# Hash-masked attention and a gated feed-forward layer on one core: bits by DVE, a third of a norm on ACT, casts and turns moved

## The chip, the cores and the metric

The kernel runs on one core of a Trainium2 chip. The metric is the time of one execution on the device, in microseconds (us), median of several runs. Five engines work side by side, each in the order of its own queue: PE (matrix products; its weight loads are PEld in the profile), DVE and POOL (element work), ACT (functions and scaled copies), and SP, which only issues transfers here. An engine waits only for the data and the buffers that its next instruction needs; what stands behind that instruction in its queue waits with it.

## The reference

Attention over 4 batches of 8 heads, 768 positions and 64 dimensions. Each position of q and k gets 6 bits, the signs of its products with a 64x6 matrix; a query sees only the keys with the same 6 bits.

```python
q_bits = (np.einsum('bhsd,dk->bhsk', q, proj) > 0)
k_bits = (np.einsum('bhsd,dk->bhsk', k, proj) > 0)
mask = q_bucket[:, :, :, None] == k_bucket[:, :, None, :]
scores = np.where(mask, scale * np.matmul(q, k.transpose(0, 1, 3, 2)), -1e9)
attn = softmax(scores)                       # with 1e-9 in the denominator
x = np.matmul(attn, v)                       # heads side by side: 3072 x 512
xn = x / np.sqrt(np.mean(x * x, -1) + 1e-6) * rms_g
g, val = xn @ w_gate, xn @ w_val             # 512 x 1536 each
out = (g * sigmoid(g) * val) @ w_out         # 1536 x 512
```

## The kernel before

The 4 batches are cut into 8 units u of 384 queries (u = 2b and 2b + 1), with 8 heads h each. A head's work is three *steps*: in step t PE computes the scores of two key blocks of the next step (`scores`, s_ps, L321), ACT takes exp of those of this step (`probs`, psb, L333), and then whatever the plan holds for the step is issued, in the order in which it was entered. There are 192 such steps. The order of heads starts with heads 0 and 1 of units 0 and 1, then heads 2 to 7 of unit 0, then of unit 1, then unit by unit; so unit 0's last head is done in step 32, and batch 1's first heads begin at step 48. The plan is a table written by hand (`at(w, s, f, ...)`: window w of 24 steps, step s), and the feed-forward products of a unit are spread by weights over the steps of the next one (`spread`).

The bits enter the scores as 6 further rows of the operands in `QK`: rows 64 to 69, of a size such that an unlike bit pushes the score down and exp makes it nothing. They come in four steps. `turn_pe` transposes a head's q or k on PE (t_ps, L148) and DVE copies it (kT, qT, L150); `cast_part` casts it into QK (L164, on POOL, or on DVE for one half of q). `hash_direct` multiplies by the 64x6 matrix for a pair of heads (d_ps, L222); `sign` takes the signs on DVE (bits, L211), once for each half of the columns. Then `send` moves the bits to the rows of QK by DMA from SP's queue (L261), two transfers a head, or `move` does it on DVE (L252), two copies a head. The bits lie in two buffers in turn, so the signs of one pair wait for the transfers of the pair before the last. Pairs 1 to 3 of batch 0 start at steps 2, 8 and 14 (`s0`), with the hash at s0 + 4; the pairs (b, hp) = (1, 0) and (1, 1) have a row of step numbers each. Later pairs are loaded as blocks of 32 columns, turned on DVE (`turn_dve`, L174 and L181), cast on POOL (`cast_pool`, L194) and hashed by `hash_one` (L202); `spots` holds their steps: load, k's turns, q's turns, hash. A helper puts off POOL's casts and v's that would come due in steps 2 to 6 of a window:

```python
def behind_norm(t):
    return t - t % NS + 7 if 2 <= t % NS < 7 else t
```

v is cast to 16 bits into `vl` (`v_prep`, L290; for pairs 1 to 3 of batch 0 on DVE). Loads of q, k and v share eight buffers, taken in turn, so that a load waits for the cast or the turn that frees its buffer, and SP's later transfers wait behind it.

`av` multiplies exp's results with v (o_ps, L346; one buffer in PSUM, two heads). After an odd head `attn_out` (`o_step`) copies o_ps out on DVE (otmp, L360), takes the reciprocal (rcp, L365), and multiplies to x (L367) and squares it (sq, L372) on POOL, or on DVE for unit 0's last pair; `sumsq` (`s_step`) sums the squares (ssp, L376). At the end of a unit `norm_scale` sums over the heads (ss, L388) and raises to the power -1/2 on POOL (rstd, L392), and `norm` scales x in three thirds of 128 rows (xn, L401). `turn_x` transposes each third as a chunk on PE (x_ps, L408) and puts it out times rms_g, on DVE (xnT, L414) or as four scalings on ACT (L412). Then come the gate and value products (g_ps and v_ps, L425), tanh on ACT (t, L433), two products on DVE (a, ht, L442 and L443), and the output projection (y_ps, L454). For unit 0 this first norm stands in steps 32 and 33 and its transposes in step 37 (`TX`), with three zero matmuls (`idle`, z_ps, L515) ahead of them; later units' norms stand in step 4 of their window. t_ps, d_ps, x_ps, g_ps, v_ps, y_ps and the sums of v (m_ps, L306, put out as cvb, L309) share three PSUM buffers in turn.

Of the kernel before, what the change touches and what calls it, by code (L numbers as in the profile page):

```python
# [33 lines left out]
def kernel(  # L34
# [12 lines left out]
    nc = tc.nc  # L47
# [110 lines left out]
    def turned(b, hp, which):  # L158
        return (qT if which == "q" else kT)[b, hp].rearrange("p (h c) -> p h c", h=2)
# [48 lines left out]
    def signs(dst, ps):  # L208

        upper = ps.bitcast(U16).rearrange("p (c two) -> p c two", two=2)[:, :, 1]  # L210
        nc.vector.tensor_scalar(  # L211
            out=dst.bitcast(U16), in0=upper, scalar1=SIGN, scalar2=BIT,
            op0=ALU.bitwise_and, op1=ALU.bitwise_or,
        )

    def hash_pairs(srcs):


        pss = [bank("d_ps", [128, HALF]) for _ in range(2)]
        for t, src in enumerate(srcs):  # L220
            for e in range(2):
                nc.tensor.matmul(  # L222
                    pss[e][32 * t : 32 * t + 32, :],
                    pj[64 * e : 64 * e + 64, 6 * e : 6 * e + 32],
                    src[64 * e : 64 * e + 64],
                    start=True, stop=True, tile_position=(64 * e, 32 * t),
                )
        return pss

    def hash_direct(b, hp, heads):  # L230

        where = [(which, hh) for hh in heads for which in "kq"]
        pss = hash_pairs([turned(b, hp, which)[:, hh, :] for which, hh in where])
        bt = spool.tile([128, S], FP16, name="bits")

        def sign(e):
            signs(bt[:, e * HALF : (e + 1) * HALF], pss[e])

        def direct(which, e):
            t = where.index((which, heads[0]))
            o = (0 if which == "q" else S) + e * HALF
            signs(
                QK[b, 2 * hp + heads[0], "h"][D:KROWS, o : o + HALF],
                pss[e][32 * t : 32 * t + 6],
            )

        def move(hh):
            for which in "kq":  # L250
                t, o = where.index((which, hh)), 0 if which == "q" else S
                nc.vector.tensor_copy(  # L252
                    QK[b, 2 * hp + hh, "h"][D:KROWS, o : o + S], bt[32 * t : 32 * t + 6, :]
                )

        def send(only=heads):
            for t, (which, hh) in enumerate(where):
                if hh not in only:
                    continue
                o = 0 if which == "q" else S  # L260
                nc.sync.dma_start(  # L261
                    out=QK[b, 2 * hp + hh, "h"][D:KROWS, o : o + S],
                    in_=bt[32 * t : 32 * t + 6, :],
                )

        return sign, direct, move, send
# [46 lines left out]
    x, xn, xnT = {}, {}, {}  # L313
# [69 lines left out]
    rstds = {}  # L383

    def norm_scale(u):

        ss = spool.tile([128, 3], FP32, name="ss")
        nc.vector.tensor_reduce(  # L388
            out=ss, in_=ssp[u % 2].rearrange("p h c -> p c h"), op=ALU.add, axis=AX.X
        )  # L390
        rstd = spool.tile([128, 3], FP32, name="rstd")
        nc.gpsimd.tensor_tensor(out=rstd, in0=ss, in1=mhalf, op=ALU.pow)  # L392
        rstds[u] = rstd

    def norm(u):
        if u not in rstds:
            norm_scale(u)
        rstd = rstds.pop(u)
        xn[u] = npool.tile([128, 3, DMODEL], FP16, name="xn")
        for c in range(3):  # L400
            nc.vector.tensor_scalar_mul(xn[u][:, c, :], x[u][:, c, :], rstd[:, c : c + 1])  # L401

    def turn_x(u, c, act=False):
        if c == 0:
# [128 lines left out]
    def at(w, s, f, *a):  # L533
        plan[NS * w + s].append(lambda: f(*a))
# [7 lines left out]
    _, direct, _, _ = hash_direct(0, 0, (0,))  # L542
# [7 lines left out]
    _, direct1, _, _ = hash_direct(0, 0, (1,))  # L550
# [5 lines left out]
        direct("q", 1)  # L556
        direct1("q", 1)

    pair_signs, moves, sends = {}, {}, {}

    def hash_only(b, hp):
        pair_signs[b, hp], _, moves[b, hp], sends[b, hp] = hash_direct(b, hp, (0, 1))

    def hash_signs(b, hp):
        for e in range(2):
            pair_signs[b, hp](e)

    def hash_pair(b, hp):
        hash_only(b, hp)
        hash_signs(b, hp)  # L570

    def send_pair(b, hp, heads=(0, 1)):
        sends[b, hp](heads)
# [7 lines left out]
    for hp, s0 in ((1, 2), (2, 8), (3, 14)):  # L581
        at(0, s0, new_pair, 0, hp)
        at(0, s0, turn_pe, 0, hp, 0, "k")
        at(0, s0 + 1, turn_pe, 0, hp, 1, "k")
        at(0, s0 + 1, cast_pool, 0, hp, "k")
        at(0, s0 + 2, turn_pe, 0, hp, 0, "q")
        at(0, s0 + 3, turn_pe, 0, hp, 1, "q")
        at(0, s0 + 3, cast_part, 0, hp, "q", 0, 0, 2, nc.vector)
        at(0, s0 + 3, cast_part, 0, hp, "q", 1)
        at(0, s0 + 4, hash_pair, 0, hp)  # L590
        if hp == 1:
            at(0, s0 + 5, send_pair, 0, hp, (1,))
            at(0, s0 + 5, move_head, 0, hp, 0)
        else:
            at(0, s0 + 5, send_pair, 0, hp)
    at(0, 1, load_natural, nc.sync, 0, 3, "k")
    at(0, 1, load_natural, nc.sync, 0, 3, "q")
    at(0, 2, load_v, nc.sync, 0, 2)
    at(0, 2, load_v, nc.sync, 0, 3)
    at(0, 8, v_prep, 0, 1, nc.vector)  # L600
    at(0, 13, v_prep, 0, 2, nc.vector)
    at(0, 19, v_prep, 0, 3, nc.vector)
    for hp, t in enumerate((4, 16, 21, 31)):
        at(0, t, v_mean, 0, hp, 2, range(6))
    for i, t in enumerate((22, 34)):
# [3 lines left out]
        at(0, 39 + 3 * i, load_w, wo, moe_w_out, 6 * i, 6)  # L609


    for hp, ts in ((0, (8, 22, 23, 24, 25, 24, 26, 26, 28, 42)), (1, (17, 27, 28, 29, 30, 29, 41, 32, 33, 43))):
        tl, ts = ts[0], ts[1:]
        for w in "kq":
            at(0, tl, load_natural, nc.sync, 1, hp, w)
        at(0, tl, load_v, nc.sync, 1, hp)
        at(0, ts[0], new_pair, 1, hp)
        for t, hh, w in zip(ts[0:4], (0, 1, 0, 1), "kkqq"):
            at(0, t, turn_pe, 1, hp, hh, w)
        at(0, ts[4], cast_pool, 1, hp, "k")  # L620
        at(0, ts[5], cast_pool, 1, hp, "q")
        if hp == 0:
            at(0, ts[6], hash_pair, 1, hp)
            at(0, ts[7], send_pair, 1, hp)
        at(0, ts[8], v_prep, 1, hp)
        at(0, ts[8], v_sum, 1, hp)

    spots = {
# [11 lines left out]
    TX = 37  # L640
# [9 lines left out]
    for n, (u, h) in enumerate(order):  # L650
        for part in range(2):
            at(0, 3 * n + 4 + part, av, u, h, part)
        if h % 2:
            if (u, h) == (0, H - 1):

                at(0, 3 * n + 5, o_step, u, h // 2, nc.vector)
                at(0, 3 * n + 5, s_step, u, h // 2)
                at(0, 3 * n + 5, norm_scale, u)
                at(0, 3 * n + 6, hash_only, 1, 1)
                at(0, 3 * n + 6, hash_signs, 1, 1)  # L660
                at(0, 3 * n + 6, norm, u)
                at(0, TX + 1, send_pair, 1, 1)
                at(0, TX - 1, idle, 2, bank)
                at(0, TX, idle, 1, bank)
                for c in range(3):
                    at(0, TX, turn_x, u, c, c == 1)
                continue
            at(0, 3 * n + 5, o_step, u, h // 2)
            at(0, 3 * n + (10 if h < 7 else 7), s_step, u, h // 2)
# [35 lines left out]
    for u in range(7):  # L705
        gates = [
            (FEED, f is gate and part == 0, [(0, f, u, ft, part)])
            for ft in range(NF) for f in (gate, value) for part in range(2)
        ]
        if u == 0:  # L710
            t0 = TX + 1
            spread(t0, 2 * NS - t0, gates)
            continue
        t0 = NS * (u + 1)
        at(0, t0 + 4, norm, u)
        pieces = []
        for i in range(9):
            c, n = divmod(i, 3)
            steps = [(0, project, u - 1, c, 4 * n, 4 * n + 4)]
            if n == 2:  # L720
                steps.append((1, store, u - 1, c))
            pieces.append((4 * PROJ, True, steps))
            if i in (6, 7):
                pieces += [
                    (TURN, False, [(0, turn_x, u, c)]) for c in ((0,), (1, 2))[i - 6]
                ]
        spread(t0, NS, pieces + gates)
# [35 lines left out]
    for c in range(2):  # L763
        project(6, c, 0, NF)
        store(6, c)
    norm(7)
    project(6, 2, 0, 4)
    for c, f0, f1 in ((0, 4, 7), (1, 7, 9), (2, 9, NF)):
# [41 lines left out]
```

## Time and profile before

| | us |
|---|---|
| median of 3 runs | 339.19 (338.9 to 339.55) |
| the profiled execution | 339.4 |
| its span, first to last instruction | 337.6 |
| PE busy in it | 329.3 (98%) |
| DVE, ACT, POOL busy | 235.8, 224.0, 149.2 |
| PE waiting for the bits' transfer, first 120 us | 1.1, once |
| PE waiting for otmp, first 120 us | 0.5, once |

The page gives each engine's busy time, the chain of work that ended last, and the costliest groups of instructions. A row of a timeline gives start, duration, engine, line, operation and tiles, and in brackets how long the engine had been idle and what ended that. Matmuls are pipelined and their ends modelled: PE may be shown busy while its next weights wait, which shows in the rows of PEld. The granted clock was 1.0 all through.

### The profile page before, as it was taken

What the parts mean: (1) busy time and instruction counts of PE and PEld (TensorE: products, weight loads), DVE (VectorE), ACT (ScalarE), POOL (GpSimd) and SP (SyncE); (2) the same over time, 40 slices, a digit from 0 to 9 for tenths busy, and PEclk for the clock granted to TensorE, in tenths of its full rate; (3) what the DMA queues carried; (4) which work ended last, traced back from release to release, by engine and by line L of the source; (5) the groups of instructions that cost most, each with busy time, mean ns of one, the idle gap of its engine ahead of it and who ended that gap; (6) DMA issues with size and microseconds to landing.
All of it is one profiled execution on the core that took longest, in us unless ns stands there. A gap on an engine that the chain in (4) does not pass through costs nothing.

```text
span 337.6 us, 7795 instructions
## 1 busy us (share of the span) xinstructions
PE 329.3 (98%) x3004; PEld 198.3 (59%) x3004; DVE 235.8 (70%) x492; ACT 224.0 (66%) x325; POOL 149.2 (44%) x201
## 2 busy tenths in 40 slices
PE   8898999999999999999999999999999999999996
PEld 4566756655566555655656556565656666664554
DVE  2898696777869558875788658884776446674870
ACT  2788886666677767777667667776667767754322
POOL 3457949427553632746373523738371121112000
PEclk9999999999999999999999999999999999999999
DMA  7944899982818527070816118000200010001002
GB/s 234 328 142 150 129 152 210 229 143 50 185 23 159 109 87 150 12 136 26 148 71 106 42 65 171 7 1 19 83 3 3 2 62 34 0 2 68 28 0 93
DMA packets 79692, 30.92 MB, mean 92 GB/s; under 512 B 64988, under 2 KB 76712, under 8 KB 79656
## 3 DMA queue, kind: packets, MB, share of 16 engines
q1 hardware_dynamic: 75528, 25.45, 31.6%
q0 software_dynamic: 3680, 4.72, 8.4%
q8 instruction: 23, 0.38, 0.5%
q10 hardware_dynamic: 448, 0.27, 0.2%
q14 instruction: 13, 0.11, 0.1%
HBM read 28.32 MB, written 6.29 MB: 103 GB/s over the span
## 4 chain that ended last, share of the span: by engine, by line
PE 91%; DVE 4%; DMA 2%; ACT 1%; issue 1%; SPq 0%; DVEq 0%
PE v_ps L425 18%; PE g_ps L425 18%; PE s_ps L321 17%; PE y_ps L454 17%; PE o_ps L346 10%; PE d_ps L202 3%; PE t_ps L148 2%; PE x_ps L408 2%; PE d_ps L222 2%; DMA qL<-in_q_dram 1%; PE z_ps L515 1%; DVE bits L211 1%; PE y_ps L473 1%; DMA QK<-bits 1%; ACT psb L333 1%
## 5 line engine op out<-in xcount | busy, mean ns | idle before, releaser
L333 ACT ACTIVATE psb<-s_ps,ebias 128x768 f16<-128x768 f32 x192 | 167.5, 899 | 25.0 <-PE s_ps L321 24.3
L321 PE MATMUL s_ps<-QK 70*128 70x384 f16 x384 | 93.9, 326 | 2.5 <-DMA QK<-bits 1.1
L433 ACT ACTIVATE t<-g_ps 128x384 f32<-128x384 f32 x96 | 47.1, 490 | 56.3 <-PE g_ps L425 56.1
L425 PE MATMUL g_ps<-xnT,wg 128*128 128x384 f16 x384 | 82.5, 325 | 0.2
L425 PE MATMUL v_ps<-xnT,wv 128*128 128x384 f16 x384 | 81.7, 325 | 0.3 <-DVE a L442 0.2
L442 DVE SCALAR_TENSOR_TENSOR a<-t,g_ps 128x384 f32<-128x384 f32 x96 | 52.8, 550 | 28.2 <-ACT t L433 26.8
L454 PE MATMUL y_ps<-wo,ht 128*128 128x512 f16 x276 | 68.0, 378 | 0.0
L367 POOL TENSOR_TENSOR x<-otmp,rcp 128x384 f32<-128x384 f32 x31 | 25.7, 829 | 93.1 <-DVE rcp L365 92.9
L346 PEld LDWEIGHTS <-psb 128*128 128x128 f16 x1152 | 52.1, 97 | 16.3 <-issue 1.3
L443 DVE SCALAR_TENSOR_TENSOR ht<-a,v_ps 128x384 f16<-128x384 f32 x96 | 53.2, 554 | 11.7 <-PE v_ps L425 3.2
L346 PE MATMUL o_ps<-vl,psb 128*128 128x65 f16 x1152 | 56.3, 193 | 0.5 <-DVE otmp L360 0.5
L321 PEld LDWEIGHTS <-QK 70*128 70x128 f16 x384 | 34.5, 98 | 36.4 <-issue 11.0
L425 PEld LDWEIGHTS <-wv 128*128 128x128 f16 x384 | 35.2, 97 | 22.6 <-issue 1.8
L425 PEld LDWEIGHTS <-wg 128*128 128x128 f16 x384 | 34.6, 97 | 21.2 <-DVE xnT L414 0.6
L454 PEld LDWEIGHTS <-ht 128*128 128x128 f16 x276 | 24.7, 97 | 22.7
L372 POOL TENSOR_TENSOR sq<-x 128x384 f32<-128x384 f32 x31 | 25.6, 826 | 2.4
L194 POOL CAST QK<-kT 64x768 f16<-64x768 f32 x20 | 16.4, 820 | 22.6 <-DVE kT L174 7.7
L466 ACT COPY ysb<-y_ps 128x512 f32<-128x512 f32 x23 | 13.5, 585 | 18.6 <-PE y_ps L454 18.6
L360 DVE TENSOR_TENSOR otmp<-o_ps,cvb 128x390 f32<-128x390 f32 x32 | 17.9, 559 | 10.0 <-PE o_ps L346 9.7
L194 POOL CAST QK<-qT 64x768 f16<-64x768 f32 x20 | 16.5, 825 | 18.5 <-DVE qT L181 17.1
L376 DVE TENSOR_REDUCE ssp<-sq 128x3 f32<-128x384 f32 x32 | 16.9, 529 | 9.9 <-POOL sq L372 9.9
L414 DVE TENSOR_TENSOR xnT<-x_ps,gcol 128x512 f16<-128x512 f16 x22 | 14.5, 685 | 5.8 <-PE x_ps L408 5.8
(71 smaller groups left out, 262.8 us busy)
## 6 DMA issues: line engine op xcount, KB each, us to landing
vn<-in_v_dram SPq DMA_DIRECT2D x16, 384.0 KB
out_dram<-ysb SPq DMA_DIRECT2D x23, 256.0 KB
qL<-in_q_dram SPq DMA_DIRECT2D x40, 96.0 KB
kL<-in_k_dram SPq DMA_DIRECT2D x40, 96.0 KB
kn<-in_k_dram SPq DMA_DIRECT2D x5, 384.0 KB
qn<-in_q_dram SPq DMA_DIRECT2D x5, 384.0 KB
wg<-in_moe_w_gate_dram POOLq DMA_DIRECT2D x2, 768.0 KB, 7.8
wv<-in_moe_w_val_dram POOLq DMA_DIRECT2D x2, 768.0 KB, 9.6
```

The source lines that it names most:

```text
L194: nc.gpsimd.tensor_copy(QK[b, 2 * hp + hh, "h"][0:64, o : o + S], src[64 * hh : 64 * hh + 64, :])
L321: nc.tensor.matmul(ps[:, j, 0:HALF], QK[b, h, "h"][0:KROWS, S + jt * 128 : S + (jt + 1) * 128], QK[b, h, "h"][0:KROWS, half * HALF : (half ...
L333: nc.scalar.activation(psb[u, h][:, 2 * ch : 2 * ch + 2, :], sps.pop((u, i))[:, :, 0:HALF], AF.Exp, bias=ebias, scale=ESCALE,)
L346: nc.tensor.matmul(o[:, c, hh, 0:65], psb[u, h][:, jt, c * 128 : (c + 1) * 128], vls[b % 2][:, h, 2 * (jt % 3) + jt // 3 if b in PARITY el ...
L360: nc.vector.tensor_add(tmp[:, :, :, 0:65], o[:, :, :, 0:65], cvb[b % 2][:, 2 * hp : 2 * hp + 2, 0:65].unsqueeze(1).to_broadcast([128, 3, 2 ...
L367: eng.tensor_mul(xd.rearrange("p c (h d) -> p c h d", h=2), tmp[:, :, :, 0:64], r.to_broadcast([128, 3, 2, 64]),)
L372: eng.tensor_mul(sq, xd, xd)
L425: nc.tensor.matmul(ps, w[:, kt, fs], xnT[u][:, kt, :], start=(kt == 0), stop=(kt == 3))
L433: nc.scalar.activation(t, fbank[u, ft, "g_ps"], AF.Tanh, scale=0.5)
L442: nc.vector.scalar_tensor_tensor(out=a, in0=t, scalar=1.0, in1=g, op0=ALU.add, op1=ALU.mult)
L443: nc.vector.scalar_tensor_tensor(out=ht[u][:, ft, :], in0=a, scalar=0.5, in1=vv, op0=ALU.mult, op1=ALU.mult)
L454: nc.tensor.matmul(y, ht[u][:, ft, c * 128 : (c + 1) * 128], wo[:, ft, :], start=(ft == 0), stop=(ft == NF - 1),)
```

## The change

- The hash of batch 1's pair 1, with its signs, leaves the first norm (step 33) for step 30; its transfers go from step 38 to 39.
- The last third of the first norm's x is scaled on ACT in step 36, and ACT puts out the transposes of chunk 2 instead of chunk 1.
- The first head of pairs 2 and 3 of batch 0 gets its bits by two DVE copies, as pair 1 had it; the second head keeps its two transfers.
- DVE's casts of v for pairs 1 to 3 of batch 0 go from steps 8, 13 and 19 to 11, 17 and 23.
- Batch 1's pairs 0 and 1 are turned, cast and hashed one to two steps sooner (pair 1's late q cast, at step 41, stays).
- Pairs (1, 2) and (1, 3) have the halves of k and q turned by DVE one or two steps sooner; the steps of their hashes stay. The steps of their casts follow the turns by the code as it is.

```diff
     def norm(u):
         if u not in rstds:
             norm_scale(u)
-        rstd = rstds.pop(u)
         xn[u] = npool.tile([128, 3, DMODEL], FP16, name="xn")
-        for c in range(3):
-            nc.vector.tensor_scalar_mul(xn[u][:, c, :], x[u][:, c, :], rstd[:, c : c + 1])
+        for c in range(3 if u else 2):
+            norm_third(u, c, nc.vector.tensor_scalar_mul)
+
+    def norm_third(u, c, mul):
+        mul(xn[u][:, c, :], x[u][:, c, :], rstds[u][:, c : c + 1])
...
         at(0, s0 + 4, hash_pair, 0, hp)
-        if hp == 1:
-            at(0, s0 + 5, send_pair, 0, hp, (1,))
-            at(0, s0 + 5, move_head, 0, hp, 0)
-        else:
-            at(0, s0 + 5, send_pair, 0, hp)
+        at(0, s0 + 5, send_pair, 0, hp, (1,))
+        at(0, s0 + 5, move_head, 0, hp, 0)
...
-    at(0, 8, v_prep, 0, 1, nc.vector)
-    at(0, 13, v_prep, 0, 2, nc.vector)
-    at(0, 19, v_prep, 0, 3, nc.vector)
+    at(0, 11, v_prep, 0, 1, nc.vector)
+    at(0, 17, v_prep, 0, 2, nc.vector)
+    at(0, 23, v_prep, 0, 3, nc.vector)
...
-    for hp, ts in ((0, (8, 22, 23, 24, 25, 24, 26, 26, 28, 42)), (1, (17, 27, 28, 29, 30, 29, 41, 32, 33, 43))):
+    for hp, ts in ((0, (8, 21, 22, 23, 24, 24, 25, 25, 27, 42)), (1, (17, 25, 26, 27, 28, 28, 41, 30, 39, 43))):
...
-        if hp == 0:
-            at(0, ts[6], hash_pair, 1, hp)
-            at(0, ts[7], send_pair, 1, hp)
+        at(0, ts[6], hash_pair, 1, hp)
+        at(0, ts[7], send_pair, 1, hp)
...
-        (1, 2): (34, (48, 48), (49, 49), 50),
-        (1, 3): (45, (57, 57), (58, 59), 60),
+        (1, 2): (34, (47, 47), (48, 48), 50),
+        (1, 3): (45, (55, 56), (57, 58), 60),
...
                 at(0, 3 * n + 5, norm_scale, u)
-                at(0, 3 * n + 6, hash_only, 1, 1)
-                at(0, 3 * n + 6, hash_signs, 1, 1)
                 at(0, 3 * n + 6, norm, u)
-                at(0, TX + 1, send_pair, 1, 1)
+                at(0, TX - 1, norm_third, 0, 2, nc.scalar.mul)
                 at(0, TX - 1, idle, 2, bank)
                 at(0, TX, idle, 1, bank)
                 for c in range(3):
-                    at(0, TX, turn_x, u, c, c == 1)
+                    at(0, TX, turn_x, u, c, c == 2)
```

The lists of ten numbers are: load, four turns (k, k, q, q), cast of k, cast of q, hash, sending, cast of v.

More of the change, by code (lines that the diff above doesn't have):

```diff
@@ L557, in second_head, with hash_pair @@
         direct1("q", 1)
[L559 to L564, printed above, removed]
+    moves, sends = {}, {}
+    def hash_pair(b, hp):
+        sign, _, moves[b, hp], sends[b, hp] = hash_direct(b, hp, (0, 1))
         for e in range(2):
[L566 to L570, printed above, removed]
+            sign(e)
     def send_pair(b, hp, heads=(0, 1)):
```

## The prediction

> **What bounds the kernel now.** I read the page first.
>
> ```profile
> PE 329.3 (98%) x3004; PEld 198.3 (59%) x3004; DVE 235.8 (70%) x492; ACT 224.0 (66%) x325; POOL 149.2 (44%) x201
> ...
> PE 91%; DVE 4%; DMA 2%; ACT 1%; issue 1%; SPq 0%; DVEq 0%
> ```
>
> PE carries the chain. The change adds and drops no matmul, so its worth is PE time lost now, less PE time lost afterwards. The second view, busy time in stretches of 4 us, has PE at 3.99 or 4.00 in every stretch from 52 to 104 us; it is short in 20 to 24 (3.51), 32 to 36 (2.94) and 44 to 48 (3.41). Third, the chain in order of time, for 0 to 55 us:
>
> ```profile
> 19.84 0.56 DVE vl L290
> 20.40 0.48 DVE otmp L360
> 20.89 0.04 issue
> 20.93 0.43 PE o_ps L346 x9
> ...
> 31.46 2.39 DMA QK<-bits
> 33.85 0.14 issue
> 33.98 0.48 PE s_ps L321 x2
> ```
>
> The cast of v (L290) stands on DVE before the copy that frees o_ps: 0.59 us. Head 6's bits come by DMA, and PE sits 1.06 us. But a PE called busy can also hide a wait. Fourth, the whole chain by time, the hashes of batch 1's last pairs beside an undisturbed one:
>
> ```profile
> 74.14 1.23 PE d_ps L202 x8
> ...
> 90.38 1.86 PE d_ps L202 x8
> ...
> 112.38 0.78 PE d_ps L202 x8
> ```
>
> Those eight matmuls need 0.78 us, and took 0.45 and 1.08 more. The weight loads say why:
>
> ```profile
> 91.40 0.14 PEld L202 LDWEIGHTS d_ps<-qT,pj 128*32 128x32 f32 x2 [0.57 <-DVE qT L174]
> ```
>
> The second q half was not yet turned. Last, the first norm on DVE:
>
> ```profile
> 45.65 0.17 DVE L388 TENSOR_REDUCE ss<-ssp 128x3 f32<-128x15 f32 x1
> 45.86 1.02 DVE L211 TENSOR_SCALAR bits<-d_ps 128x384 uint16<-128x384 uint16 x2
> 46.90 1.43 DVE L401 TENSOR_SCALAR xn<-x,rstd 128x512 f16<-128x512 f32 x3
> ```
>
> POOL's rstd runs from 45.97 to 46.87. The two signs lie in its shadow: removing them frees 0.02 us.
>
> **The change, first stretch (to 50 us).** Times below are of the profiled execution; "step" is the plan's number. I follow PE from the first edit, spacing instructions as the DVE and PE timelines do (DVE: copy 0.45, sign 0.47, move 0.37, row reduction 0.46, uncovered cast 0.48; PE: scores 0.33, three transposes 0.33, nine o_ps 0.27, hash 0.81 to 0.89).
>
> Steps 8 to 13. Without the cast otmp ends at 20.28, not 20.87; o_ps starts at 20.34, 0.59 sooner. The cast now stands before pair 2's signs. It took 0.82 here, with POOL casting, so the signs start at 23.6 (23.54 before). Two moves follow, 0.73 by the pair at 18.51. The row reduction starts at 25.38 instead of 25.30 and otmp at 26.31 instead of 26.22, and o_ps and m_ps wait for that queue. The 0.59 is gone: PE is within 0.1 of its old times at step 17, and at step 20 too, as pair 3's hash waits for DVE's q copy (28.71, before 28.73).
>
> Steps 18 to 24. The cast ahead of pair 3's signs costs 0.2 to 0.4 there, the moves 0.73, and otmp ends at 32.69 instead of 32.22. The bits are in place at 31.65, so head 6's scores start at 33.02, behind nine o_ps that waited 0.05 for otmp: 0.96 sooner than 33.98.
>
> Steps 24 to 32. In this replay DVE has not been idle since 23; two k copies, the last v cast and two q copies stand between it and the hash of batch 1's pair 0, which comes one step sooner. Its last operand is ready near 35.5 and PE leaves it at 36.3, having lost 0.45. PE's path from head 6's scores to the last o_ps of head 7 was 8.60 (33.98 to 42.58). It becomes 8.60, less 0.33 (one triple of transposes already done), plus 0.81 (the hash of pair 1, formerly behind that o_ps, now ahead), plus 0.45, plus 0.15 for another otmp: 9.68, from 33.02 to 42.70. That is 0.1 late. The hash was free where it stood: there PE filled its time with zero matmuls (L515).
>
> The norm. From the last o_ps to xn the chain (otmp, x, sq, sums, rstd) keeps its 4.3 us: xn starts at 47.0. Two thirds on DVE end at 48.0 (47.94 was the second's end). ACT has no row for this third; the nearest are the 128x512 copy at 0.585 and the 128x128 scaling at 0.25 to 0.37, so 0.5 to 0.7. It waits at ACT's head for rstd, with probs of step 37 behind it: that exp, 46.26 to 47.16 before, ends near 48.4. Nobody needs it before 48.8. But ACT now turns chunk 2, the last that PE transposes: its four scalings (1.14 us) start near 48.75 instead of 48.49 and end at 49.9, where DVE is done at 49.3. The first gate matmul, at 49.67 before, starts at 49.9. First stretch: **+0.25**, bounds -0.25 (casts uncovered, chunk 2 early) and +0.75 (casts at their slowest row 0.90, chunk 2 at 49.1).
>
> The Trainium skill speaks against this edit: "ScalarE: Activation LUTs", section "Rules for kernel authors", gives multiplications to VectorE. The trace agrees so far: 0.47 us for a third on DVE, 0.585 for the nearest copy on ACT. By the rule the third would end on DVE at 48.5, the gate start at 49.8 and the first stretch stand at +0.1; by the rows of ACT's queue it is the +0.25.
>
> **SP and the loads.** The k load of batch 1's pair 0 takes the buffer of the v that is now cast at 23.6: it is issued near 23.7 instead of 20.17. Three such loads kept the queues busy from 21.2 to 25.1, so now to 28.7, with pair 2's two remaining bit transfers among them. Pair 3's, in the same position, landed 1.2 us after the loads' last packet. That gives 29.9; PE needs them at 30.15. Free by 0.25, and beyond it one for one. The k turn, from 31.7, has its data. The transfers of batch 1's pair 1, held to step 39, are not needed before step 54. The loads behind them start 1.4 sooner.
>
> **Hash of (1, 2), 74 us.** The turns start where they did (DVE ends its last gate product at 71.1 either way), but the q half no longer waits behind a 0.41 reduction: done at 74.08, and the hash loses 0.04 instead of 0.45. Gain 0.41. The price is on POOL:
>
> ```profile
> 75.25 0.83 POOL L367 TENSOR_TENSOR x<-otmp,rcp 128x384 f32<-128x384 f32 x1 [0.80 <-DVE rcp L365]
> 76.15 0.83 POOL L372 TENSOR_TENSOR sq<-x 128x384 f32<-128x384 f32 x1
> 77.99 0.87 POOL L392 TENSOR_TENSOR rstd<-ss,mhalf 128x3 f32<-128x3 f32 x1 [1.01 <-DVE ss L388]
> 78.83 1.78 POOL L194 CAST QK<-qT 64x768 f16<-64x768 f32 x2
> ```
>
> With q's last turn at step 48 its casts come due at 49, no longer put behind the norm; in the changed order they stand ahead of x. x starts at 76.15 instead of 75.25, rstd at 78.75, xn at 79.66 instead of 78.90. The casts of v then run beside xn, so I keep xn's slow 1.03 (a third takes 0.43 with POOL idle, as at 120 us). The first transposes get their operand at 80.7, where PE, 0.41 early, would be at 80.32. PE waits 0.4: the gain is spent. Net **0.0**, bounds -0.41 (xn at 0.43) and +0.3 (the third chunk late too).
>
> The Trainium skill ("SBUF — State Buffer", "Who interferes with whom") calls the pair of ports that DVE shares with POOL a lock, held for a whole instruction. By it xn's first third would wait out a 0.9 cast and end near 80.95, making the net +0.2 where the row makes it 0.0. The 1.03 beside POOL and 0.43 alone agree with it.
>
> **Hash of (1, 3), 90 us.** The first k half goes ahead of otmp, and each later half one gate earlier. DVE: k at 84.05, otmp 84.75, k 85.45, product 86.15 (before 86.03; its bank is needed at 87.2), q at 87.3 and 89.2, done at 90.0. The hash stands at 90.33. Its wait goes: **-1.07**, bounds -1.1 and -0.8. otmp 0.7 later hurts nobody: the next o_ps is at 86.61. PE has no idle time of size after that which is tied to a transfer, so the gain stays.
>
> **Sum.** +0.25 + 0.0 - 1.07 = -0.8. The profiled execution took 339.4, 337.6 of it span; it becomes 338.6. The median of the runs, 339.19, lies 0.2 below it, so **338.4**.
>
> **The rivals.** *All the waits go*: 0.59 + 1.06 at the start, 0.41 and 1.07 at the hashes, less the 0.81 of the moved hash: -2.3, 336.9, or as far towards it as DVE lets the start go. For it: each is a row. Against it: DVE is busy 3.97 of 4 us from 24 to 28 and gets 1.46 of moves on top. 22%.
>
> *The start eats more*: +0.75 there, 338.9. For it: casts at 0.90 and the late chunk on ACT are both rows. 18%.
>
> *DVE becomes the bound of the start, and the kernel slower.* If what enters its queue from 23 to 36 us lands fully on PE: moves 1.46, three casts at 0.82 instead of 0.48 (1.0), the hash 0.81, the late chunk 0.25; less the 0.59 and 1.06: +1.9. With -1.07 that is +0.8, 340.0. It turns slower from +1.75 on. For it: DVE had only 0.34 idle before each pair's signs. Against it: DVE idled 1.59 before 34.83, while PE waited for the bits. 10%.
>
> **How the numbers follow.** About 0.2%, 0.7 us, is what a measurement of this kernel can tell from no change. My forecast has 50%, between 337.9 and 338.8; 0.36 of it I put beyond 0.7 us (below 338.5) and 0.14 short of it. Faster: 0.36 and the first rival's 0.22, 0.58. Same: 0.14 and 0.18, 0.32. Slower: 0.10. The range, 337.0 to 339.3, leaves out the lower end of the first rival and the slower one.
>
> **What would show it.** Right: scores of head 6 near 33.0 with no wait for bits; the d_ps piece of the chain near 90 us at 0.78; xn of the second norm about 0.8 later against its otmp; first gate matmul at 49.7 to 50.2. Wrong: the first gate matmul before 49.2 or after 50.6, or the (1, 3) hash still at 1.8.

## The result and the profile after

| | before | after |
|---|---|---|
| median, us (22 runs each, on the same chips) | 339.26 | 340.19 |
| ratio after to before, 95% interval | | 1.0024 [1.0014, 1.0035] |
| profiled execution; its span, us | 339.4; 337.6 | 340.21; 338.4 |

The kernel became slower by 0.9 us, where 338.4 was forecast.

To find where, I subtract the start times of the same PE instruction in the two traces. The first scores come 0.22 sooner in after, and so do all up to the first edit, which has nothing to do with the change: executions differ by up to 1.1 there. So all that follows is counted from each execution's own first scores. Even then a stretch that is the same in two kernels came out up to 0.3 apart.

| stretch | predicted | measured |
|---|---|---|
| up to the first gate matmul | +0.25 | +1.42 |
| hash of (1, 2) | -0.41 | -0.44 |
| second norm | +0.41 | +1.02 |
| hash of (1, 3) | -1.07 | -1.20 |
| sum | -0.8 | +0.8 |

The page of after, engines and chain, in which PE's share of the chain fell:

```profile
PE 327.8 (97%) x3004; PEld 197.4 (58%) x3004; DVE 237.4 (70%) x495; ACT 224.7 (66%) x326; POOL 149.1 (44%) x201
...
PE 78%; DVE 8%; DMA 8%; POOL 2%; issue 1%; ACT 1%; SPq 0%; ACTq 0%; DVEq 0%; POOLq 0%
```

DVE's share of the chain doubled. (Most of the DMA share is one transfer of kL that landed ahead of the turns of (1, 2); the hash behind it came sooner than before, so it is no cause.) The busy time in stretches of 4 us (span, PE, PEld, DVE, ACT, POOL, then clock and DMA) shows the place, first in before and then in after:

```profile
20.00:24.00 4.00, 3.51 (x55) 2.17 (x54) 3.74 (x8) 2.95 (x5) 2.67 (x3) 1.00 0.66 220
24.00:28.00 4.00, 3.94 (x53) 3.28 (x49) 3.97 (x10) 3.35 (x5) 2.83 (x4) 1.00 0.25 89
...
32.00:36.00 4.00, 2.94 (x36) 2.51 (x35) 1.94 (x6) 2.79 (x4) 3.13 (x4) 1.00 0.11 31
```

```profile
20.00:24.00 4.00, 3.98 (x59) 2.55 (x58) 3.88 (x8) 3.42 (x5) 3.30 (x4) 1.00 0.76 233
24.00:28.00 4.00, 2.90 (x38) 2.13 (x35) 3.89 (x10) 2.55 (x4) 1.53 (x3) 1.00 0.34 90
...
32.00:36.00 4.00, 3.24 (x44) 2.76 (x42) 3.92 (x10) 2.99 (x5) 1.92 (x3) 1.00 0.02 7
```

From 20 to 24 PE has the gain that was expected (3.98 for 3.51). From 24 to 28 it loses more than that (2.90 for 3.94), and from 32 to 36 DVE is as full as it can be (3.92 for 1.94). The tables of PE's waits in the first 60 us name them, first before and then after: the wait for the bits is gone, and one for a buffer that DVE's copy of k frees and a longer one for otmp stand in its place.

```profile
PE s_ps L321 <- DMA QK<-bits: 1.1, 1, 1.1
...
PE o_ps L346 <- DVE otmp L360: 0.5, 1, 0.5
```

```profile
PE m_ps L306 <- DVE kT L150: 1.1, 1, 1.1
...
PE o_ps L346 <- DVE otmp L360: 0.8, 1, 0.8
```

The chain in order of time (start, us, what) runs through DVE there:

```profile
22.70 1.09 DVE vl L290
23.80 0.94 DVE bits L211 x2
24.76 0.71 DVE QK L252
25.49 0.35 DVE QK L252
25.87 0.55 DVE ssp L376
26.42 0.47 DVE kT L150
26.89 0.48 DVE otmp L360
```

The cast of v has 1.17 where 0.82 was put, the pair of moves 1.07 where 0.73 was put. POOL's timeline beside it tells why:

```profile
22.24 1.15 POOL L164 CAST QK<-kT 64x768 f16<-64x768 f32 x1
...
24.44 0.82 POOL L164 CAST QK<-qT 64x768 f16<-64x768 f32 x1
```

The cast of v, from 22.63 to 23.80, ends 0.41 after POOL's cast, which ended at 23.39; the first move, 24.76 to 25.47, ends 0.21 after the later POOL cast, which ended at 25.26. The second move, with POOL idle, takes 0.35.

At 90 us the hash has lost its wait, as forecast:

```profile
92.05 0.78 PE d_ps L202 x8
```

### The profile page after: what moved, and what is told of

Same layout as the page of the kernel before. It is cut to its first block, busy times and chain, and to the rows that moved or that the text cites. A ratio compares the mean times of both kernels' runs of the same rounds, so it can differ in the third digit from the quotient of the medians.

```text
span 338.4 us, 7787 instructions
## 1 busy us (share of the span) xinstructions
PE 327.8 (97%) x3004; PEld 197.4 (58%) x3004; DVE 237.4 (70%) x495; ACT 224.7 (66%) x326; POOL 149.1 (44%) x201
## 4 chain that ended last, share of the span: by engine, by line
PE 78%; DVE 8%; DMA 8%; POOL 2%; issue 1%; ACT 1%; SPq 0%; ACTq 0%; DVEq 0%; POOLq 0%
PE v_ps L427 16%; PE g_ps L427 16%; PE s_ps L321 15%; PE y_ps L456 15%; PE o_ps L346 9%; DMA kL<-in_k_dram 5%; PE d_ps L202 2%; PE x_ps L410 1%; PE t_ps L148 1%; PE d_ps L222 1%; DMA pj<-in_proj_dram 1%; DVE xn L403 1%; POOL QK L194 1%; DVE ssp L376 1%; PE y_ps L475 1%
## 5 line engine op out<-in xcount | busy, mean ns | idle before, releaser
L376 DVE TENSOR_REDUCE ssp<-sq 128x3 f32<-128x384 f32 x32 | 16.9, 529 | 11.3 <-POOL sq L372 11.2
```

The source lines that it names most:

```text
L376: nc.vector.tensor_reduce(out=ssp[u % 2][:, hp, :], in_=sq, op=ALU.add, axis=AX.X)
```

## The experiments

Each kernel was compared with the kernel before on the same chip (its median stands behind the stroke). "xn" and "gate" are the starts of the first norm's scaling and of the first gate matmul, in us later than before, counted from the first scores.

| run | median / before | ratio, 95% interval | xn | gate |
|---|---|---|---|---|
| after | 340.19 / 339.26 | 1.0024 [1.0014, 1.0035] | +1.76 | +1.42 |
| 1 turns sooner only | 338.92 / 339.48 | 0.9976 [0.9957, 0.9995] | +0.15 | +0.15 |
| 2 the same, q cast late | 338.25 / 339.48 | 0.9962 [0.9934, 0.999] | +0.04 | +0.04 |
| 3 start only | 341.19 / 339.48 | 1.0035 [1.0014, 1.0056] | +1.81 | +1.47 |
| 4 after, v casts back | 340.37 / 339.48 | 1.0019 [1.0002, 1.0036] | +2.12 | +1.78 |
| 5 after, no new moves | 340.07 / 339.44 | 1.0024 [0.9997, 1.0051] | +1.92 | +1.58 |
| 6 after, third on DVE | 340.66 / 339.44 | 1.0037 [1.002, 1.0055] | +1.77 | +1.77 |
| 7 after, v casts behind otmp | 340.26 / 339.44 | 1.0019 [1.0, 1.0038] | +1.68 | +1.34 |
| 9 after, hash in the norm | 340.18 / 339.44 | 1.0006 [0.9975, 1.0036] | +1.80 | +1.46 |
| 13 run 2 and the third on ACT | 337.65 / 339.32 | 0.996 [0.9933, 0.9987] | +0.30 | -0.04 |
| 14 after, pairs back | 340.13 / 339.32 | 1.0018 [0.9999, 1.0038] | +1.63 | (+2.43) |
| 15 moves only | 341.29 / 339.32 | 1.0047 [1.0028, 1.0067] | +1.90 | +1.90 |
| 16 early pairs only | 340.10 / 339.32 | 1.0021 [0.9999, 1.0044] | +0.67 | +0.67 |
| 17 v casts only | 339.88 / 339.62 | 1.0 [0.9971, 1.0029] | +0.78 | +0.78 |
| 18 run 14, loads early | 339.21 / 339.62 | 0.9977 [0.9955, 1.0] | +0.63 | +0.29 |
| 19 run 13, move of pair 3, loads early | 337.36 / 339.62 | 0.992 [0.9894, 0.9946] | -0.13 | -0.47 |
| 20 after, loads early | 340.01 / 339.42 | 1.001 [0.9995, 1.0025] | +1.69 | +1.35 |

### The later part alone (runs 1 and 2)

Run 1 is the kernel before with the two new rows of `spots` and nothing else. Run 2 also puts the q casts of (1, 2) behind the norm:

```diff
-            at(0, behind_norm(turns[-1] + 1), cast_pool, b, hp, w)
+            late = (b, hp, w) == (1, 2, "q")
+            at(0, 55 if late else behind_norm(turns[-1] + 1), cast_pool, b, hp, w)
```

> The kernel before with the earlier turns of (1, 2) and (1, 3) alone. Theory A (POOL's order delays the second norm by itself): the two hashes give back 0.44 and 1.2, the second norm loses 1.0 behind the q casts, sum -0.6 us. Rival B (the second norm was late only because it inherited the late start): no loss there, -1.6 us.

> As e1, but POOL's two q casts of (1, 2) put off to step 55, behind the second norm. A: the hash gains stay and the norm's loss goes, -1.6 us against the kernel before, 1.0 less than e1. B: the same time as e1. A third possibility: the casts beside xn slow it, as in the kernel before, and nothing more.

In run 1 the three pieces were -0.44, +1.05 and -1.21: those of after, with the start untouched. In run 2 they were -0.44, +0.13 and -1.21. POOL's timeline of after in the second norm, and then that of run 2:

```profile
75.73 1.70 POOL L194 CAST QK<-qT 64x768 f16<-64x768 f32 x2
77.52 0.83 POOL L367 TENSOR_TENSOR x<-otmp,rcp 128x384 f32<-128x384 f32 x1
...
80.12 0.87 POOL L392 TENSOR_TENSOR rstd<-ss,mhalf 128x3 f32<-128x3 f32 x1 [0.88 <-DVE ss L388]
80.97 0.81 POOL L290 CAST vl<-vn 128x768 f16<-128x768 f32 x1
81.75 1.17 POOL L296 TENSOR_TENSOR vadd<-vn 128x384 f32<-128x384 f32 x1
```

```profile
75.14 0.83 POOL L367 TENSOR_TENSOR x<-otmp,rcp 128x384 f32<-128x384 f32 x1 [0.74 <-DVE rcp L365]
...
78.59 1.78 POOL L194 CAST QK<-qT 64x768 f16<-64x768 f32 x2
```

In after the casts stand ahead of x; in run 2 x starts as soon as rcp is there (0.74 idle ahead of it) and the casts follow rstd. So nearly all of the loss in the second norm is the order on POOL: 0.92 of 1.05 by the traces. (The medians are 0.67 apart, and the intervals of the two ratios overlap.)

### Does the rest of the kernel catch the start up? (run 3)

After with the old two rows of `spots`.

> The changed kernel with the turns of (1, 2) and (1, 3) as before. A: the first gate matmul stays as late as in the changed kernel (1.4 us of loss up to there) and nothing is won back later: +1.4 us. Rival (the start is innocent and its lateness is caught up in slack behind it): within 0.3 us of the kernel before.

It does not: the gate is +1.47, and the last products (y_ps) still are +1.5.

### One part of the start taken back (runs 4, 5, 6, 7 and 9)

Run 4 puts the casts of v back to steps 8, 13 and 19; run 7 puts them to 9, 15 and 21, behind the otmp of those steps; run 5 sends both heads of pairs 2 and 3 by DMA again; run 9 puts the hash of (1, 1) back to step 33.

> The changed kernel with DVE's v casts back at steps 8, 13 and 19. If the casts' place beside POOL's casts is the larger cost (they took 1.17 there instead of 0.56 to 0.90): signs 0.6 to 1.1 sooner, first gate matmul 0.5 to 1.0 sooner than in the changed kernel. If the moves' own time fills DVE's queue: the otmp copies of steps 14 and 20 stay as late, the gain of step 8 (0.47) is lost, and the gate comes within 0.3 of the changed kernel's.

> The changed kernel with pairs 2 and 3 sending both heads' bits by DMA again. If the moves fill DVE's queue (0.35 each, 0.71 beside a POOL cast, two pairs: 2.1 us): otmp of steps 14 and 20 come 1 and 2 us sooner, head 6 waits for its bits again (scores within 0.3 of 34.0), and the first gate matmul comes 0.8 to 1.3 sooner than in the changed kernel. If the casts of v beside POOL's casts are the cost: 0.3 or less.

> The changed kernel with DVE's v casts at steps 9, 15 and 21, just behind otmp, where POOL runs x and sq and no casts. If a cast beside a POOL cast costs 0.5 more (1.17 against 0.56 to 0.7): two of the three casts shorter, signs 0.5 sooner, gate 0.5 to 1.0 sooner than in the changed kernel. If only the number of DVE instructions counts: gate unchanged within 0.2.

> The changed kernel with the hash of batch 1's pair 1 back in the first norm (step 33). By the prediction's step (0.81 of PE work put ahead of the last o_ps): gate 0.6 to 0.8 sooner than in the changed kernel. Rival (ACT's row of exps or DVE's queue sets the last o_ps, PE's hash lies beside it): 0.2 or less.

None takes the start back: +1.34 to +1.78 against +1.42. With the casts back the moves meet POOL's casts later and take 1.49 and 1.35 a pair. With the moves gone head 6 waits for its bits again, and its scores are as late as in after within 0.4. In run 7 the first two casts of v stand beside POOL's x instead of its casts and take 1.04 each, so they are not short there either.

Run 9 gives back only 0.30 of the 0.81 that the prediction gave to the hash of (1, 1): from head 6's scores to head 7's last o_ps PE takes 9.34 for 9.64, since scores now wait there for ACT's exp. And the sum ahead of the last otmp then waits for POOL's sq, so that xn starts as late as in after (why, runs 14, 18 and 20 show). The rows of PE and of DVE in run 9:

```profile
42.08 0.48 PE L321 MATMUL s_ps<-QK 70*128 70x384 f16 x2 [0.45 <-ACT psb L333]
...
43.60 0.56 DVE L376 TENSOR_REDUCE ssp<-sq 128x3 f32<-128x384 f32 x1 [0.35 <-POOL sq L372]
```

Run 6 scales the third on DVE again and lets ACT put out chunk 1:

```diff
-        for c in range(3 if u else 2):
+        for c in range(3):
...
-                at(0, TX - 1, norm_third, 0, 2, nc.scalar.mul)
-                    at(0, TX, turn_x, u, c, c == 2)
+                    at(0, TX, turn_x, u, c, c == 1)
```

> The changed kernel with the whole first norm on DVE and chunk 1 put out by ACT, as before. By the prediction's step (chunk 2 on ACT holds the gate): gate 0.2 sooner than in the changed kernel. By the trace after (from xn's start to the gate 2.43 us instead of 2.77): gate 0.3 later.

The gate came 0.35 later. PE's timeline of after, and then that of run 6:

```profile
48.98 0.40 PE L410 MATMUL x_ps<-ident,xn 128*128 128x128 f16 x4 [0.67 <-DVE xn L403]
...
50.87 0.84 PE L427 MATMUL g_ps<-xnT,wg 128*128 128x384 f16 x4
```

```profile
48.57 0.40 PE L410 MATMUL x_ps<-ident,xn 128*128 128x128 f16 x4 [0.68 <-DVE xn L403]
...
50.79 0.81 PE L427 MATMUL g_ps<-xnT,wg 128*128 128x384 f16 x4
```

From the first transpose to the gate it is 1.89 in after and 2.22 in run 6 (2.22 in before too). ACT's timeline of after shows the third and its four scalings:

```profile
48.44 0.72 ACT L403 ACTIVATE xn<-x,rstd 128x512 f16<-128x512 f32 x1 [0.88 <-POOL rstd L392]
...
50.19 1.14 ACT L414 ACTIVATE xnT<-x_ps,gcol 128x128 f16<-128x128 f16 x4 [0.24 <-PE x_ps L410]
```

The gate starts at 50.87, before the last of the four ends at 51.33: its first matmul needs the first of them (50.56) and DVE's second chunk, which ends at 50.71. In before DVE's chunk ended at 49.52 and the gate started at 49.67: 0.15 behind DVE, and 0.16 in after. A third less on DVE is what the gate gets.

### One part of the start done alone (runs 13, 15, 16 and 17)

Run 13 adds the third on ACT to run 2. Run 15 is before with the moves of pairs 2 and 3, run 16 before with batch 1's pairs 0 and 1 sooner (the hash of (1, 1) stays in the norm), run 17 before with the casts of v at 11, 17 and 23.

> The kernel before with the turns of (1, 2) and (1, 3) sooner, the q casts of (1, 2) put to step 55, and the third of the first norm on ACT with chunk 2 put out by ACT. Theory: the third gains 0.35 by itself, as the kernels with and without it differed (first gate matmul 0.35 sooner), and the later part gains 1.45, so 1.8 us in all, about 337.6 by the median and a ratio near 0.9947. Rival, the prediction's own step: the third costs 0.15 to 0.25 where DVE is not late, since ACT's scalings of chunk 2 end after DVE's; then the gate comes 0.2 later and the sum is 1.25, about 338.2.

> The kernel before with only the moves: the first head of pairs 2 and 3 of batch 0 gets its bits by two DVE copies. Theory F: the moves end head 6's wait of 1.06 but the two copies beside POOL's casts cost 1.06 a pair on DVE, so the first gate matmul comes 0.3 to 0.8 late and the run is 339.7 to 340.2. Rival E: the moves by themselves do no harm, the gate is within 0.3 of before or up to 0.6 sooner, and the run 338.8 to 339.6.

> The kernel before with only the steps of batch 1's pairs 0 and 1 sooner (turns at 21 to 28, the hash of pair 0 at 25; the hash of pair 1 stays in the first norm, its signs at step 33 with it). Theory E: head 6's scores still wait for their bits, and behind them more work lies ahead of unit 0's last o_ps; the first gate matmul is 0.7 to 1.0 late and the run near 340.2. Rival F: nothing to be seen, within 0.3, near 339.3.

> The kernel before with only the three casts of v later (steps 11, 17, 23). Theory (each edit of the start trades one wait for another): o_ps at step 12 comes 0.5 sooner, but the cast, now 1.17 beside POOL's casts, stands ahead of each pair's signs, so pair 3's signs and with them the transfer for head 6 come 0.4 to 0.8 late; the first gate matmul is 0.2 to 0.8 late and the run 339.5 to 340.1. Rival: the casts by themselves are a gain that the other edits eat; the gate 0.2 to 0.5 sooner, the run 338.8 to 339.1.

The third: xn to gate is 2.43 for 2.77, as in after. That is read from the stretch alone: the ratios of runs 2 and 13 (0.9962 and 0.996) do not tell the two kernels apart. The moves cost most, 1.9, more than either theory gave. The chain of run 15:

```profile
24.08 0.58 DVE QK L252
24.67 0.01 issue
24.68 0.89 DVE QK L252
25.57 0.03 issue
25.60 0.56 DVE vl L290
26.16 0.46 DVE ssp L376
26.62 0.48 DVE kT L150
27.09 0.04 issue
27.14 0.51 PE m_ps L306 x6
```

Here both moves meet POOL; the second ends at 25.57, 0.21 after POOL's cast at 25.35. PE loses 1.07 at once at m_ps. At pair 3 the moves end the wait for the bits, but otmp now makes o_ps wait 1.0, and nothing is won.

The early pairs cost 0.67 and the casts 0.78 by the trace, about as their theories had them; the median of run 17 (+0.26, interval to both sides) does not settle the latter. Singly the four edits come to 1.90 + 0.67 + 0.78 - 0.34 = +3.0, together to +1.42: they do not add up.

### Two paths that are late together (runs 14, 18 and 20)

Run 14 is after with the steps of batch 1's pairs as before. Run 18 also moves POOL's first loads of w_gate and w_val (1.00 and 0.80 of POOL) to step 19, where POOL waits 2.0 for rcp. Run 20 is after with only these loads moved.

```diff
-        at(0, t, load_w, wg, moe_w_gate, 0, 4, cols)
-        at(0, t + 3, load_w, wv, moe_w_val, 0, 4, cols)
+        at(0, t if i else 19, load_w, wg, moe_w_gate, 0, 4, cols)
+        at(0, t + 3 if i else 19, load_w, wv, moe_w_val, 0, 4, cols)
```

> The kernel after with the steps of batch 1's pairs 0 and 1 as they were before (turns at 22 to 30, hashes at 26 and 33, transfers of pair 1 at 39); moves, casts of v, the third and the later turns stay changed. Measured from the first scores, the first gate matmul was 1.42 late in the kernel after. Theory E (the pairs' earlier turns and hash push PE and DVE work ahead of unit 0's last o_ps): it falls to 0.4 to 0.7, and the run to about 339.4. Rival F (DVE is full from 23 to 36 us because of the moves and the casts beside POOL, and the order of the pairs hardly matters): it stays at 1.2 to 1.5, about 340.1.

> The kernel with batch 1's first pairs as before (all else as after), and POOL's two loads of w_gate and w_val, 1.00 and 0.80, moved from steps 22 and 25 to step 19, where POOL waits 2.0 for rcp. Theory P (the lateness reaches the first norm through POOL's queue: otmp of step 20 late, so x, sq and all behind them, and unit 0's last otmp stands behind a sum that waits 0.9 for sq): that wait goes, otmp comes 0.8 sooner against the last o_ps, and the run is 0.6 to 0.9 under that of the kernel without this edit, near 339.4. Rival: DVE itself or PE is late, and nothing changes, 340.1.

> The kernel after with only POOL's loads of w_gate and w_val moved to step 19. Theory: two paths to the first norm are late by the same amount, POOL's queue (x, sq, the sum ahead of otmp) and PE's own (the earlier turns and the hash of batch 1's pairs ahead of unit 0's last o_ps); taking away one alone gives nothing, as putting the pairs back alone gave nothing, so the first gate matmul stays 1.2 to 1.5 late and the run near 340.2. Rival: POOL's queue alone is the path, the gate comes 0.6 to 1.0 sooner, the run near 339.4.

In run 14 PE went from head 6's scores to the last o_ps of head 7 in 8.60 again (9.64 in after), and yet xn was as late. (Its gate is in brackets because the granted clock fell to 0.50 from 49 to 52 us in that one execution; xn starts ahead of it.) DVE's timeline of run 14, and then that of run 18:

```profile
43.23 0.56 DVE L376 TENSOR_REDUCE ssp<-sq 128x3 f32<-128x384 f32 x1 [0.92 <-POOL sq L372]
43.70 0.55 DVE L360 TENSOR_TENSOR otmp<-o_ps,cvb 128x390 f32<-128x390 f32 x1
```

```profile
42.34 0.54 DVE L376 TENSOR_REDUCE ssp<-sq 128x3 f32<-128x384 f32 x1
43.00 0.57 DVE L360 TENSOR_TENSOR otmp<-o_ps,cvb 128x390 f32<-128x390 f32 x1
```

In run 14 unit 0's last otmp stands on DVE behind the sum of the pair before, and that waits 0.92 for POOL's sq. POOL is late because otmp of step 20 was late (32.94 for 31.68, though its first scores were 0.82 sooner), and x, sq, a load, two casts, a load, two casts, x and sq follow one another there with hardly a gap. Take the loads out of that queue and otmp waits for o_ps alone. Taking one path away gives xn +1.63 (pairs) or +1.69 (loads); both together give +0.63, and the ratio goes from 1.0018 and 1.001 to 0.9977. The late otmp goes to the norm by POOL's queue, the early pairs by PE's, and each hides the other. What is left in run 18 is the lateness that head 6's scores already had there (+0.64).

### A faster version (run 19)

Run 13 with the moves for pair 3 alone (`hp == 1` becomes `hp != 2`) and the loads at step 19.

> The fastest version so far (turns sooner, late q cast, third on ACT) with the moves for pair 3 alone and POOL's two weight loads at step 19. By the traces the moves of pair 2 cost 1.07 at step 17 and those of pair 3 nothing, since they end head 6's wait for its transfer (1.06 to 1.4) while otmp then makes o_ps wait 0.5 to 1.0. Theory: 0.3 to 0.6 sooner than without, 337.1 to 337.4. Rival: the moves of pair 3 delay otmp of step 20 by their 1.1 to 1.4, PE waits for that as long as it did for the transfer, and nothing is gained or up to 0.5 lost, 337.6 to 338.1.

The gate comes 0.43 sooner than in run 13, all of it at head 6, where PE's timeline now has

```profile
33.08 0.43 PE L346 MATMUL o_ps<-vl,psb 128*128 128x65 f16 x9 [0.92 <-DVE otmp L360]
```

in place of a wait of 1.4 for the bits. 337.36 us, ratio 0.992, is the fastest of the kernels; runs 13 and 19 ran on different occasions, so between them only the traces are compared.

## Why the prediction was wrong

**Steps 8 to 13: here the sum failed.** The 0.59 came (0.47 at the next scores), but the replay then put the cast at 0.82 and the moves at 0.73, rows taken where POOL began or ended otherwise or was idle. They took 1.17 and 1.07: +0.69. The row reduction stood at 26.09 (0.22 added to the trace's 25.87) instead of 25.38, and at step 17 PE was 0.58 behind the old times instead of within 0.1.

**Steps 18 to 24: the same two rows again.** Otmp ended at 34.28 (0.22 added) instead of 32.69, head 6's scores came at 34.60 instead of 33.02. No bits were waited for, as forecast, but o_ps waited 0.8 for otmp instead of 0.05. So 1.58 of lateness lies in two terms, the cast and the moves beside POOL.

The rule was at hand: the Trainium skill, "SBUF — State Buffer", section "Who interferes with whom", lets whichever of DVE and POOL comes first keep the ports that they share for a whole instruction. The traces agree: nine casts and moves of DVE ended a fixed time behind POOL's instruction (below). The prediction weighed it for xn alone and sized the casts and moves by rows.

**Steps 24 to 32: the sum right, its terms not.** 9.68 from head 6's scores to head 7's last o_ps; 9.64 measured, and 8.60 with the pairs back. But the hash of (1, 1) was worth 0.30 of its 0.81 (run 9), and the earlier turns without it 0.67 (9.27 in run 16), where the other terms, -0.33, 0.45 and 0.15, make 0.27. So the two errors cancelled, by luck. The loads were not waited for, as forecast, but not for the reason given: the k load of batch 1's pair 0, put at 23.7, was issued at 20.17 by the old times (19.95 in after), so it did not wait for the late cast of v. What the replay did not see is POOL's queue, late by as much: without the 1.04 of the pairs nothing would have been won (run 14).

**The norm.** Last o_ps to xn took 4.42 (4.3 forecast). The third on ACT took 0.72, just over the 0.5 to 0.7 given. The step that failed is the gate waiting for the last of ACT's four scalings: it waits for the first, and for DVE. By the replay's own 49.3 for DVE it would have gained. So a loss of 0.15 to 0.2 was a gain of 0.34. "ScalarE: Activation LUTs" of the Trainium skill, section "Rules for kernel authors", would leave this multiplication on VectorE; one third indeed took longer on ACT (0.72, for 0.48 and 0.64 of the two on DVE), and the stretch to the gate still became 0.34 shorter, because DVE was the one waited for.

In sum, from +0.25 to +1.42: 1.58 from the cast and the moves, -0.04 to the last o_ps, +0.12 to xn, -0.47 from xn to the gate.

**Hash of (1, 2) and second norm.** The gain of 0.41 was right (0.44). The order on POOL was right too: x at 76.30 by the old times, where 76.15 was forecast. But xn came at 79.81 instead of 79.66, its second third took 1.22 beside vadd (1.17 on POOL) instead of 1.03, and the third chunk's transposes came at 84.45, right behind DVE's first xnT, which ended at 84.39: PE lost 1.02 instead of 0.41. The lock's own result, +0.2 net, was nearer to the +0.58 than the 0.0 by rows, and the remedy is run 2.

**Hash of (1, 3).** Right: -1.20 for -1.07.

**The rivals.** The third, DVE as the bound of the start, is what happened, at +1.42 of its +1.9. That its total of +0.8 was met is luck: the start was 0.48 below its sum, in which the moved hash and the late chunk were too dear, and the second norm cost 0.58 more than the 0.0 it reckoned with. Without that the traces' sum would be +0.22, too little to be called slower. Its "0.34 idle before each pair's signs" was not so for pair 2, where DVE had 0.14 (23.40 to 23.54). It was given 10% because DVE had 1.59 idle before 34.83. That idle time was there while PE waited for the bits, and the moves and the casts, 0.89 longer at pair 3 than reckoned (1.58 less 0.69), took it.

## What to carry to other kernels

Price a copy, a cast or a scaling of DVE that neither reads nor writes PSUM at its new place by the cast or product that POOL runs there, not by a row from elsewhere: begun under that one, it ended a fixed time after it in every trace here. When an edit takes a wait from PE, follow the late result through the queues of the helper engines too, to the next point where all meet; two queues may be late alike, and then undoing one part shows nothing and only the pair does. When a producer is moved sooner, look at what its consumers now stand ahead of.

## What the runs showed of the hardware

- A move on DVE (6x768 f16) takes 0.35 alone. Begun beside a POOL cast it ended 0.21 after POOL's end, in all 26 cases of the 18 traces (25.47 behind 25.26 and 32.64 behind 32.43 in after; 24.67 behind 24.46 and 25.57 behind 25.35 in run 15; 30.60 behind 30.39 and 31.50 behind 31.29 in run 19).
- The cast of v (128x768 f16) takes 0.56 alone; begun beside a cast or product of POOL it ended 0.41 or 0.42 after POOL's end, in all 34 cases (23.80 behind 23.39 and 30.97 behind 30.55 in after, 25.38 behind 24.96 in before).
- A third of xn (128x512, f32 to f16), begun beside a cast or product of POOL, ended 0.28 or 0.29 after POOL's end, in all 54 cases (79.93 behind 79.65, 80.90 behind 80.62 and 81.86 behind 81.58 in before; 82.06 behind 81.78 and 83.20 behind 82.91 in after).
- It holds the other way too. POOL's 64x768 cast took 0.81 to 0.85 with none of these three beside it, nor a cast of DVE into QK; begun under one of them it ended 0.68 to 0.70 after DVE's end (24.49 behind 23.80 in after, 26.06 behind 25.38 in before) and took up to 1.21.
- Not every pair does this. DVE's row sum (L376) in before, 25.30 to 25.84, ran through under POOL's cast of 24.91 to 26.06; and in run 19 the cast of v, 31.53 to 32.09, took its 0.56 under POOL's load of w_gate, 31.24 to 32.42.
- Of the 18 profiled executions, in run 14's alone the granted clock was 0.50 for 3 us, and xn to gate took 3.57 instead of 2.43. What set it off, no run shows.
